# Half of a cosine FFN's first product by one level of Strassen's recursion, in pairs of token blocks

## The chip, the core and the metric

The kernel runs on one core of a Trainium2 chip. The time is the device time of one execution in microseconds (us). PE is TensorE's matrix multiplication (PEld its loading of weights), DVE is VectorE, ACT is ScalarE, POOL is GpSimd, and SP is SyncE, which issues most DMAs here. PSUM is the matmuls' output memory, of eight banks with 512 fp32 values for each of 128 partitions; SBUF is the working memory; DRAM here is the chip's own large memory. Matmul operands are fp32r, a shortened fp32 that TensorE multiplies in one pass.

## The reference

Sparse attention over 8 batches, 8 heads, 576 positions of 64 values, and a feed-forward part on its output of 4608 tokens by 512:

```python
scores = q @ k.T / sqrt(64)
mask_local   = (0 <= i - j) & (i - j < 32)        # heads 0 to 3
mask_strided = (0 <= i - j) & (i % 32 == j % 32)  # heads 4 to 7
attn = softmax(where(mask, scores, -1e9))
x = (attn @ v)           # heads side by side: 4608 x 512
h = x @ w_in             # 512 x 2048
g = h * cos(h)
out = g @ w_out          # 2048 x 512
```

## The kernel before

The feed-forward part works on blocks of 384 tokens, twelve in all (`j` from 0), and for each block on 16 chunks `f` of 128 hidden values. A step (`chunk(j, f)`) is one pair (block, chunk). Every fp32 operand is held as a high part, rounded to fp32r, and a low part, the rest; a product is high × high + low × high + high × low. `hidden` makes the first product: 4 slices of 128 inputs by 3 matmuls, twelve 384-wide matmuls into a bank `h` (L420). Then comes a chain that changes engines: ACT counts the turns of 2π (L426), DVE takes them off (L427), ACT makes the sine, with the quarter turn that makes a cosine of it (L430), DVE multiplies it by h (L433), ACT rounds the high part `g_hi` (L436), POOL takes the low part `g_lo` (L437). `outer` makes the second product: 3 tiles of 128 tokens by 3 matmuls, nine 512-wide matmuls into `acc0` to `acc2` (L444). It runs LAG = 3 steps behind `hidden`, so that the chain has three steps' time. After a block's last chunk ACT and DVE copy the three sums to `o` (L452, L454), and SP writes them out (L455).

All weights are converted at the start and in block 0 (L135 to L154) and stay in SBUF as `wi_h`, `wi_l`, `wo_h`, `wo_l`.

Attention is cut into units, seven a batch: three local ones (L277 scores, L286 a transpose on DVE, L298 products) and four strided ones (L328 scores, L344 transposes on PE, L358 products). The local products fill two banks, copied out by ACT (L306) and DVE (L310). Batches 0 and 1 come ahead of the feed-forward part and feed blocks 0 and 1 from SBUF. The 42 units of batches 2 to 7 are laid over the steps of blocks 2 to 11 by the table `KNOTS`; they write their result to `xT` in DRAM, from which `load_x` takes each later block (L399, split at L389 and L390). Two units' stretches make a `burst` ahead of a step's first product: the products of one unit and the scores of a later one, interleaved matmul by matmul where both use the same tile shape. Three banks (`acc0` to `acc2` of the pool `ps`) are attention's own, two are `h`'s, three are the sums'.

The matmuls of blocks 2 to 11 stand in the order in which they are written (`in_turn`); a scheduler sets the order of each other engine's queue at build time, and an engine takes its queue in that order. A DMA of SP waits in SP's queue until what it needs is there.

Of the kernel before, what the change touches and what calls it, by code (L numbers as in the profile page):

```python
# [74 lines left out]
def attention_cos_ffn(ctx, tc, qkl, vl, qkvs, w_in, w_out, eye, eye16, mask_l0, mask_l, mask_s, out):  # L75
# [40 lines left out]
    wi_h = const.tile([P, NFC, NKC, P], F32R, name="wi_h")  # L116
    wi_l = const.tile([P, NFC, NKC, P], F32R, name="wi_l")
    wo_h = const.tile([P, NFC, DM], F32R, name="wo_h")
    wo_l = const.tile([P, NFC, DM], F32R, name="wo_l")
# [59 lines left out]
    class Attention:  # L179
# [134 lines left out]
        def strided(self, b, p, u):  # L314
# [9 lines left out]
            mask = ms.unsqueeze(1).broadcast_to([P, SU, GB])  # L324
            s_ps = self.score_bank(mask)

            def score(t, i):
                self.scored = self.pe(nc.tensor.matmul(  # L328
                    s_ps[half(1 - i, GB), t * GB:(t + 1) * GB], q_t[half(i), t], k_t[half(i), t],
# [86 lines left out]
    def hidden(j, f, x_hi, x_lo):  # L416
        h = ps_h.tile([P, 512], F32, name="h")[:, :TB]
        ops = [(w, x, c) for c in range(NKC) for w, x in ((wi_h, x_hi), (wi_h, x_lo), (wi_l, x_hi))]
        for i, (w, x, c) in enumerate(ops):
            mm = nc.tensor.matmul(h, w[:, f, c], x[c], start=(i == 0), stop=(i == len(ops) - 1))  # L420
# [19 lines left out]
    def outer(j, f, g_hi, g_lo, acc):  # L440
        for t in range(NTT):
            ts = slice(t * P, (t + 1) * P)
            for i, (g, w) in enumerate(((g_hi, wo_h), (g_hi, wo_l), (g_lo, wo_h))):
                mm = nc.tensor.matmul(  # L444
                    acc[t], g[:, ts], w[:, f], start=(f == 0 and i == 0), stop=(f == NFC - 1 and i == 2)
# [228 lines left out]
```

## Time and profile before

| | |
|---|---|
| runs | 946.0, 948.48, 949.2 us; median 948.48 |
| profiled execution | span 945.8 us; the page gives its span only, and the fastest run, 946.0, is 0.2 us longer |
| PE | 928.2 us busy, 98% of the span, 8020 matmuls |
| PEld / ACT / DVE / POOL | 87% / 50% / 46% / 39% |
| DMA | 75.55 MB, 80 GB/s over the span |
| first products, L420 | 768 × 3 matmuls of 384 |
| second products, L444 | 576 × 3 matmuls of 512 |

A group's row reads: line, engine, operation, output<-inputs, shapes, xcount, then after the bar the busy time and the mean ns of one, then the idle time of that engine just ahead of them and what ended it. A row in order of time reads: start, duration, engine, line, operation, output<-inputs, and in brackets the idle time ahead of it and the instruction whose end released it. In a row by windows, the busy times of PE, PEld, DVE, ACT and POOL are followed by PEclk (the TensorE clock granted, 1 is full), the DMA engines' busy share, and GB/s. A DMA row ends with KB each and the median us from issue to landing.

### The profile page before, as it was taken

What the parts mean: (1) busy time and instruction counts of PE and PEld (TensorE: products, weight loads), DVE (VectorE), ACT (ScalarE), POOL (GpSimd) and SP (SyncE); (2) the same over time, 40 slices, a digit from 0 to 9 for tenths busy, and PEclk for the clock granted to TensorE, in tenths of its full rate; (3) what the DMA queues carried; (4) which work ended last, traced back from release to release, by engine and by line L of the source; (5) the groups of instructions that cost most, each with busy time, mean ns of one, the idle gap of its engine ahead of it and who ended that gap; (6) DMA issues with size and microseconds to landing.
All of it is one profiled execution on the core that took longest, in us unless ns stands there. A gap on an engine that the chain in (4) does not pass through costs nothing. (4 is left out here: it accounts for less than half of the span.)

```text
span 945.8 us, 19478 instructions
## 1 busy us (share of the span) xinstructions
PE 928.2 (98%) x8020; PEld 818.7 (87%) x8020; DVE 435.2 (46%) x885; ACT 468.8 (50%) x947; POOL 365.3 (39%) x382
## 2 busy tenths in 40 slices
PE   9899999999999999999999999999999999999998
PEld 5678899998888888888989888888998889999997
DVE  5657756446554444343344443534444444323222
ACT  3556777465555544545445543544445543433433
POOL 2636655535443353323343343423243334223221
PEclk9679999999999999999999999999999999999999
DMA  8634433123423222111213232112211311000000
GB/s 306 209 101 146 148 134 112 34 99 120 119 60 112 64 72 88 60 42 58 86 43 104 60 93 68 61 38 66 82 47 60 98 33 42 34 1 26 34 1 34
DMA packets 40265, 75.55 MB, mean 80 GB/s; under 512 B 4848, under 2 KB 22768, under 8 KB 40176
## 3 DMA queue, kind: packets, MB, share of 16 engines
q1 hardware_dynamic: 31680, 66.21, 22.2%
q10 hardware_dynamic: 8496, 8.09, 2.5%
q8 instruction: 63, 1.03, 0.5%
q14 instruction: 26, 0.21, 0.1%
HBM read 56.98 MB, written 17.30 MB: 79 GB/s over the span
## 5 line engine op out<-in xcount | busy, mean ns | idle before, releaser
L437 POOL TENSOR_TENSOR g_lo<-r,g_hi 128x384 fp32r<-128x384 f32 x192 | 198.9, 1036 | 439.0 <-issue 237.1
L420 PE MATMUL h<-x_hi,wi_h 128*128 128x384 f32 x768 | 264.2, 344 | 4.9 <-DVE r L433 4.8
L420 PE MATMUL h<-x_hi,wi_l 128*128 128x384 f32 x768 | 259.0, 337 | 0.0
L420 PE MATMUL h<-x_lo,wi_h 128*128 128x384 f32 x768 | 258.1, 336 | 0.0
L444 PE MATMUL acc<-wo_h,g_hi 128*128 128x512 f32 x576 | 228.1, 396 | 1.0 <-DVE o L452 1.0
L427 DVE SCALAR_TENSOR_TENSOR r<-r,h 128x384 f32<-128x384 int32 x192 | 105.7, 550 | 265.7 <-ACT r L426 265.5
L444 PE MATMUL acc<-wo_l,g_hi 128*128 128x512 f32 x576 | 226.7, 394 | 0.0
L444 PE MATMUL acc<-wo_h,g_lo 128*128 128x512 f32 x576 | 222.7, 389 | 0.0
L426 ACT ACTIVATE r<-h 128x384 int32<-128x384 f32 x192 | 93.4, 486 | 153.0 <-PE h L420 146.1
L430 ACT ACTIVATE r<-r,biases 128x384 f32<-128x384 f32 x192 | 118.3, 616 | 99.6 <-DVE r L427 97.9
L420 PEld LDWEIGHTS h<-x_hi,wi_h 128*128 128x128 f32 x768 | 144.4, 188 | 17.0 <-DVE r L433 7.8
L420 PEld LDWEIGHTS h<-x_lo,wi_h 128*128 128x128 f32 x768 | 144.5, 188 | 5.5
L436 ACT CAST g_hi<-r 128x384 fp32r<-128x384 f32 x192 | 98.4, 512 | 93.2 <-DVE r L433 91.9
L420 PEld LDWEIGHTS h<-x_hi,wi_l 128*128 128x128 f32 x768 | 144.2, 188 | 0.1
L433 DVE TENSOR_TENSOR r<-r,h 128x384 f32<-128x384 f32 x192 | 105.9, 552 | 81.9 <-ACT r L430 81.5
L444 PEld LDWEIGHTS acc<-wo_h,g_lo 128*128 128x128 f32 x576 | 108.1, 188 | 24.2
L444 PEld LDWEIGHTS acc<-wo_h,g_hi 128*128 128x128 f32 x576 | 108.0, 188 | 18.6 <-DVE o L452 1.8
L444 PEld LDWEIGHTS acc<-wo_l,g_hi 128*128 128x128 f32 x576 | 108.4, 188 | 14.7
L390 POOL TENSOR_TENSOR x_lo<-x_lo,x_hi 128x384 fp32r<-128x384 f32 x40 | 41.9, 1051 | 49.6 <-DVE x_hi L389 37.2
L242 ACT ACTIVATE e_sb<-t_sb,biases 128x324 f32<-128x324 f32 (+1 forms) x42 | 24.6, 586 | 57.7 <-POOL t_sb L233 42.7
L389 DVE CAST x_hi<-x_lo 128x384 fp32r<-128x384 f32 x40 | 22.7, 575 | 53.2 <-DMA x_lo<-xT 53.0
L233 POOL TENSOR_TENSOR t_sb<-t_sb,mx 128x324 f32<-128x324 f32 (+1 forms) x42 | 32.4, 771 | 18.3 <-DVE mx L232 18.3
(74 smaller groups left out, 737.6 us busy)
## 6 DMA issues: line engine op xcount, KB each, us to landing
qk<-in_qkvs SPq DMA_DIRECT2D x32, 324.0 KB, 3.7
qk<-in_qkl SPq DMA_DIRECT2D x24, 416.0 KB, 4.4
out<-o SPq DMA_DIRECT2D x36, 256.0 KB, 2.2
raw<-in_w_in SPq DMA_DIRECT2D x16, 512.0 KB, 4.3
raw<-in_w_out SPq DMA_DIRECT2D x16, 512.0 KB, 3.6
x_lo<-xT SPq DMA_DIRECT2D x40, 192.0 KB, 2.5
v<-in_vl SPq DMA_DIRECT2D x24, 224.0 KB, 3.1
xT<-x_l ACTq DMA_DIRECT2D x40, 96.0 KB, 3.0
```

Of the source, the lines that this page charges most:

```text
L233: nc.gpsimd.tensor_tensor(out=t, in0=t, in1=mx[:, :n].unsqueeze(2).broadcast_to([P, n, w]), op=ALU.subtract)
L242: nc.scalar.activation(out=e, in_=t, func=AF.Silu, bias=shift1, scale=0.0625)
L389: copy(out=hi, in_=x)
L390: nc.gpsimd.tensor_tensor(out=lo, in0=x, in1=hi.bitcast(F32), op=ALU.subtract)
L420: mm = nc.tensor.matmul(h, w[:, f, c], x[c], start=(i == 0), stop=(i == len(ops) - 1))
L426: nc.scalar.activation(out=k, in_=h, func=AF.Copy, scale=1.0 / (2.0 * math.pi), bias=0.25)
L427: red = nc.vector.scalar_tensor_tensor(out=r, in0=k, scalar=-2.0 * math.pi, in1=h, op0=ALU.mult, op1=ALU.add)
L430: sin = nc.scalar.activation(out=r, in_=r, func=AF.Sin, bias=quarter)
L433: nc.vector.tensor_tensor(out=r, in0=r, in1=h, op=ALU.mult)
L436: nc.scalar.copy(out=g_hi, in_=r)
L437: nc.gpsimd.tensor_tensor(out=g_lo, in0=r, in1=g_hi.bitcast(F32), op=ALU.subtract)
L444: mm = nc.tensor.matmul(acc[t], g[:, ts], w[:, f], start=(f == 0 and i == 0), stop=(f == NFC - 1 and i == 2))
```

## The change

Blocks 0 to 3 stay as they are (`PLAIN` = 4). Blocks 4 to 11 are worked off as four pairs. For a pair (2 × 384 tokens) and a "quad" q (chunks q and q + 8), the first product is a 2 × 2 product of blocks: hidden halves by input halves of 256, and input halves by token halves. One level of Strassen's recursion in Winograd's form makes it with 7 products in place of 8. Each is 2 slices by 3 matmuls, six 384-wide matmuls: 42 for a quad in place of 48.

- Seven combined weights are made for each of 8 quads, while blocks 2 and 3 run (`combine`): four are sums, made by POOL and DVE, split by ACT and POOL; three are plain ones. All, and `w_out`'s parts, are written to DRAM (`wis`, `wos`). In blocks 4 to 11 they are read back for each quad of each pair (`load_quad`, 2.88 MB), two quads ahead. The resident weights' memory is released at block 4.
- Seven combined token operands are made for each pair (`stage_x`) and split (`split_operand`: 14 casts on ACT, 7 subtractions each on DVE and POOL). For later pairs this lies in the last quad of the pair before.
- Six banks hold the pair's sums `acc0` to `acc5`, two (`a`, `b`) are left. The seven products accumulate in these; four results (c11, c22, c21, c12) leave them by an ACT copy or a DVE addition into SBUF and go through the same chain (`curved`).
- The second product's 12 outer tiles of the quad before (3 matmuls of 512 each) are put between the seven products, 2, 2, 2, 2, 2, 1 and 1 of them.
- Attention: batches 2 to 4 (21 units) and the two units in flight are laid over blocks 2 and 3 (16 burst slots in 16 steps, then 7 in 11). Batches 5 to 7 (21 units, 12 strided and 9 local) go one to a quad, in `a` and `b`: scores behind the third product, transposes ahead of the seventh, products at the end, each a stretch of its own.

```diff
-KNOTS = ((3, 0), (13, 9), (29, 15), (61, 23), (77, 29), (109, 37), (125, 43), (141, 44))
+KNOTS = ((3, 0), (19, 16), (30, 23))
+PLAIN = 4
+FILL = (2, 2, 2, 2, 2, 1, 1)
...
+    def combine(sp, q):
...
+        def formed(i, x, y, op):
+            t = sp.tile([P, 2 * P], F32, name="sf", bufs=3)
+            nc.vector.tensor_tensor(out=t, in0=x, in1=y, op=op)
+            part = sp.tile([P, 2, 2 * P], F32R, name="sr", bufs=2)
+            nc.scalar.copy(out=part[:, 0], in_=t)
+            nc.gpsimd.tensor_tensor(out=part[:, 1], in0=t, in1=part[:, 0].bitcast(F32), op=ALU.subtract)
+            nc.sync.dma_start(out=wis[q][i], in_=part.bitcast(F32))
...
+            if n >= LAG + 1 and (n - LAG - 1) % 3 == 0 and (n - LAG - 1) // 3 < NQ:
+                combine(sp, (n - LAG - 1) // 3)
         while pend:
             outer(*pend.pop(0))
+    plain.close()
...
+        def stage_x(c):
+            at = (PLAIN + 2 * c) * TB
+            held = {}
+            for name, k, n in (("b12", 0, 1), ("b11", 0, 0), ("b22", 1, 1), ("b21", 1, 0)):
+                held[name] = xr.tile([P, 2, TB], F32, name=name)
+                nc.sync.dma_start(out=held[name], in_=xT[:, 2 * k:2 * k + 2, at + n * TB:at + (n + 1) * TB])
+            b12, b11, b22, b21 = held.values()
+            t1, t2, t4 = (xr.tile([P, 2, TB], F32, name=name) for name in ("t1", "t2", "t4"))
+            nc.vector.tensor_tensor(out=t1, in0=b12, in1=b11, op=ALU.subtract)
+            nc.vector.tensor_tensor(out=t2, in0=b22, in1=t1, op=ALU.subtract)
+            nc.gpsimd.tensor_tensor(out=b12, in0=b22, in1=b12, op=ALU.subtract)
+            nc.gpsimd.tensor_tensor(out=t4, in0=b21, in1=t2, op=ALU.subtract)
+            return t2, b11, b21, b12, t1, t4, b22
+
+        def split_operand(i, raw):
+            hi, lo = (xo.tile([P, 2, TB], F32R, name=f"{name}{i}") for name in ("xo_hi", "xo_lo"))
+            for k in range(2):
+                nc.scalar.copy(out=hi[:, k], in_=raw[:, k])
+                engine = nc.vector if k else nc.gpsimd
+                engine.tensor_tensor(out=lo[:, k], in0=raw[:, k], in1=hi[:, k].bitcast(F32), op=ALU.subtract)
+            return hi, lo
+
+        def load_quad(q):
...
+                ws.append(wr.tile([P, 2, 2, P], F32R, name="wq", bufs=20))
...
+                wos_.append(wr.tile([P, 2, DM], F32R, name="wo", bufs=7))
...
+        def products(unit):
+            att.banks = [(ps, "a"), (ps, "b")]
...
+        raws = stage_x(0)
+        operands = [split_operand(i, raw) for i, raw in enumerate(raws)]
+        loaded = {n: load_quad(n % NQ) for n in range(2)}
+        for n in range(total):
...
+            last = q == NQ - 1 and c + 1 < NPAIR
+            if last:
+                raws = stage_x(c + 1)
+            def use(i, to, start, stop):
+                product(to, w[i], operands[i], start, stop)
+                if last:
+                    operands[i] = split_operand(i, raws[i])
+            b = bank("b")
+            use(0, b, True, False)
+            fill(FILL[0])
+            a = bank("a")
+            use(1, a, True, False)
+            nc.scalar.copy(out=p1, in_=a)
+            nc.vector.tensor_tensor(out=u2, in0=b, in1=p1, op=ALU.add)
+            fill(FILL[1])
+            use(2, a, False, True)
+            nc.scalar.copy(out=c11, in_=a)
+            made.append((q, 0, 0, curved(c11)))
+            fill(FILL[2])
+            if n < len(units):
+                scores(units[n])
+            use(3, b, False, False)
+            nc.vector.tensor_tensor(out=u3, in0=b, in1=p1, op=ALU.add)
+            fill(FILL[3])
+            a = bank("a")
+            use(4, a, True, False)
+            nc.vector.tensor_tensor(out=c22, in0=a, in1=u3, op=ALU.add)
+            made.append((q + NQ, 1, 1, curved(c22)))
+            fill(FILL[4])
+            use(5, b, False, True)
+            nc.vector.tensor_tensor(out=c21, in0=b, in1=p1, op=ALU.add)
+            made.append((q + NQ, 1, 0, curved(c21)))
+            fill(FILL[5])
+            if unit:
+                turned(unit)
+            use(6, a, False, True)
+            nc.vector.tensor_tensor(out=c12, in0=a, in1=u2, op=ALU.add)
+            made.append((q, 0, 1, curved(c12)))
+            fill(FILL[6])
+            if unit:
+                products(unit)
```

The order of the queues shows three places. In these rows a name's number tells buffers apart, and brackets give the semaphores waited for. First SP, at the step from one block to the next. Before, `out_0<-o` writes a block's sums and `x_lo<-xT` loads the operand of the block after next:

```order
L399 DMA x_lo_5019<-xT_96 128x384 [waits PE_49,Pool_49]
L399 DMA x_lo_5020<-xT_96 128x384 [waits DMAHW5_49,PE_49,Pool_49]
L268 DMA v_4344<-in_vl 128x448 [waits DMAHW6_49,PE_49]
L317 DMA qk_4735<-in_qkvs 128x648 [waits DMAHW3_49,DMAHW1_49,PE_49]
L399 DMA x_lo_5021<-xT_96 128x384 [waits DMAHW7_49,DMAHW2_49,Pool_49]
L399 DMA x_lo_5022<-xT_96 128x384 [waits DMAHW3_49,DMAHW0_49,Pool_49]
L455 DMA out_0<-o_4481 128x512 [waits DMAHW4_49,Activation_49]
L455 DMA out_0<-o_4487 128x512 [waits DMAHW5_49,DVE_49]
L455 DMA out_0<-o_4493 128x512 [waits DMAHW6_49,Activation_49]
```

In the changed kernel, at the step from block 3 to the first pair, `b12` to `b21` are the first pair's operands and `wq` its first weights:

```order
L282 DMA v_5687<-in_vl 128x448
L471 DMA out_0<-o_5108 128x512 [waits Activation_49]
L652 DMA b12_5167<-xT_159 128x2x384
L471 DMA out_0<-o_5114 128x512 [waits DVE_49]
L471 DMA out_0<-o_5120 128x512 [waits DMAHW2_49,Activation_49]
L652 DMA b11_5169<-xT_159 128x2x384 [waits DMAHW3_49]
L652 DMA b22_5171<-xT_159 128x2x384 [waits DMAHW4_49]
L652 DMA b21_5173<-xT_159 128x2x384 [waits DMAHW5_49]
L673 DMA wq_5224<-wis0_160 128x512 [waits DMAHW6_49]
```

Before, the loads of the next block's operand stand ahead of the writes of the sums; now three of the four stand behind them.

Second POOL, at a change of blocks. Before (`pn_s` and `t_sb` are a softmax's, L390 splits the next block's operand):

```order
L437 TENSOR_TENSOR g_lo_5962<-r_5956,g_hi_5961 128x384 [waits PE_49,Activation_49,Pool_49]
L437 TENSOR_TENSOR g_lo_5993<-r_5987,g_hi_5992 128x384 [waits PE_49,Activation_49,Pool_49]
L233 TENSOR_TENSOR t_sb_6033<-t_sb_6033,mx_6034 128x324 [waits DVE_49]
L437 TENSOR_TENSOR g_lo_6067<-r_6061,g_hi_6066 128x384 [waits PE_49,Activation_49,Pool_49]
L390 TENSOR_TENSOR x_lo_6692<-x_lo_6692,x_hi_6688 128x384 [waits DMAHW1_49,DVE_49]
L253 TENSOR_TENSOR pn_s1_89<-e_sb_6038,z_6043 128x6x54 [waits DVE_49]
L437 TENSOR_TENSOR g_lo_6107<-r_6101,g_hi_6106 128x384 [waits PE_49,Activation_49,Pool_49]
L437 TENSOR_TENSOR g_lo_6138<-r_6132,g_hi_6137 128x384 [waits PE_49,Activation_49,Pool_49]
```

After, at the step to the first pair (`xo_lo0` to `xo_lo6` are the low parts of the seven operands, `xo_lo0` that of the first product):

```order
L453 TENSOR_TENSOR g_lo_5044<-r_5038,g_hi_5043 128x384 [waits PE_49,Activation_49,Pool_49]
L453 TENSOR_TENSOR g_lo_5075<-r_5069,g_hi_5074 128x384 [waits PE_49,Activation_49,Pool_49]
L666 TENSOR_TENSOR xo_lo1_5189<-b11_5169,xo_hi1_5188 128x384 [waits DMAHW3_49,Activation_49]
L657 TENSOR_TENSOR b12_5167<-b22_5171,b12_5167 128x768 [waits DMAHW4_49,DMAHW0_49,DVE_49]
L666 TENSOR_TENSOR xo_lo4_5207<-t1_5175,xo_hi4_5206 128x384 [waits Activation_49]
L666 TENSOR_TENSOR xo_lo6_5219<-b22_5171,xo_hi6_5218 128x384 [waits Activation_49]
L658 TENSOR_TENSOR t4_5177<-b21_5173,t2_5176 128x768 [waits DMAHW5_49,DVE_49]
L666 TENSOR_TENSOR xo_lo2_5195<-b21_5173,xo_hi2_5194 128x384 [waits Activation_49]
L666 TENSOR_TENSOR xo_lo0_5183<-t2_5176,xo_hi0_5182 128x384 [waits Activation_49]
L666 TENSOR_TENSOR xo_lo3_5201<-b12_5167,xo_hi3_5200 128x384 [waits Activation_49]
L666 TENSOR_TENSOR xo_lo5_5213<-t4_5177,xo_hi5_5212 128x384 [waits Activation_49]
```

Before, one split of the next block's operand stands among the low parts `g_lo` of running steps; now nine operations stand in a row behind the last `g_lo`, and `xo_lo0` is the seventh of them.

Third DVE, where a local unit's products are copied out. Before (`x_l<-acc1` is the copy):

```order
L251 RECIPROCAL z_6043<-z_6043 128x6 [waits DVE_49]
L427 SCALAR_TENSOR_TENSOR r_6101<-r_6101,h_6088 128x384 [waits Activation_49,Pool_49]
L433 TENSOR_TENSOR r_6101<-r_6101,h_6088 128x384 [waits Activation_49]
L427 SCALAR_TENSOR_TENSOR r_6132<-r_6132,h_6119 128x384 [waits Activation_49]
L433 TENSOR_TENSOR r_6132<-r_6132,h_6119 128x384 [waits Activation_49]
L310 COPY x_l_6151<-acc1_6153 128x192 [waits DMAHW2_49,PE_49]
L231 TENSOR_TENSOR t_sb_6210<-acc0_2449,ml_75 128x384 [waits PE_49]
L232 TENSOR_REDUCE mx_6211<-t_sb_6210 128x6 [waits DVE_49]
```

After, in the last quad of a pair (L793 and L801 make c21 and c12, L693 and L695 are the chain's two DVE operations, `x_l<-b` is the copy):

```order
L793 TENSOR_TENSOR h_6619<-b_6476,p1_6496 128x384 [waits PE_49]
L695 TENSOR_TENSOR r_6598<-r_6598,h_6596 128x384 [waits Activation_49]
L264 TENSOR_SCALAR z_6569<-z_6569 128x6 [waits DVE_49]
L265 RECIPROCAL z_6569<-z_6569 128x6 [waits DVE_49]
L693 SCALAR_TENSOR_TENSOR r_6621<-r_6621,h_6619 128x384 [waits Activation_49,Pool_49]
L801 TENSOR_TENSOR h_6639<-a_6589,u2_6497 128x384 [waits PE_49]
L300 STREAM_TRANSPOSE pt_l_6574<-e_sb_6564 128x384 [waits Pool_49]
L695 TENSOR_TENSOR r_6621<-r_6621,h_6619 128x384 [waits Activation_49]
L693 SCALAR_TENSOR_TENSOR r_6641<-r_6641,h_6639 128x384 [waits Activation_49]
L695 TENSOR_TENSOR r_6641<-r_6641,h_6639 128x384 [waits Activation_49]
L324 COPY x_l_6654<-b_6656 128x192 [waits DMAHW6_49,PE_49]
```

In both the copy stands behind the multiply that follows a sine (L433, now L695 on c12's `r_6641`). Before, it empties a bank of attention's own; now it empties `b`, which the next quad's first product fills.

More of the change, by code (lines that the diff above doesn't have):

```diff
@@ L114, in order @@
         )
[L116 to L119, printed above, removed]
+    wp = plain.enter_context(tc.tile_pool(name="wp", bufs=1, reuse_waits="tile"))
+    wi_h, wi_l, wo_h, wo_l = [], [], [], []
+    for f in range(NFC):
+        for held, name, shape in (
+            (wi_h, "wi_h", [P, NKC, P]), (wi_l, "wi_l", [P, NKC, P]), (wo_h, "wo_h", [P, DM]), (wo_l, "wo_l", [P, DM]),
+        ):
+            held.append(wp.tile(shape, F32R, name=f"{name}{f}"))
+    xs = plain.enter_context(tc.tile_pool(name="xs", bufs=2 * NKC, reuse_waits="tile"))
     xT = dram.tile([P, NKC, NTOK], F32, name="xT")
+    wis = [dram.tile([7, P, 2, 2 * P], F32, name=f"wis{q}") for q in range(NQ)]
+    wos = [dram.tile([P, 2, DM], F32, name=f"wos{f}") for f in range(NFC)]
     def load_weight(cv, src, hi, lo, after, scalar):
@@ L162, in need_weights @@
             load_weight(
-                cv, w_in.bitcast(I32)[f], wi_h[:, f].rearrange("p c n -> p (c n)"),
-                wi_l[:, f].rearrange("p c n -> p (c n)"), after, False,
+                cv, w_in.bitcast(I32)[f], wi_h[f].rearrange("p c n -> p (c n)"),
+                wi_l[f].rearrange("p c n -> p (c n)"), after, False,
             )
-            load_weight(cv, w_out.bitcast(I32)[f], wo_h[:, f], wo_l[:, f], after, True)
+            load_weight(cv, w_out.bitcast(I32)[f], wo_h[f], wo_l[f], after, True)
             weights = f + 1
@@ L201, in bank @@
         def bank(self, kind):
-            pool, name = next(kind)
+            pool, name = self.banks.pop(0) if self.banks else next(kind)
             return pool.tile([P, 512], F32, name=name)
@@ L215, in score_bank @@
                 return bank
+            if self.banks:
+                return self.bank(None)
             n = next(self.turns)
@@ L324, in strided @@
             mask = ms.unsqueeze(1).broadcast_to([P, SU, GB])
+            rows = GP if self.banks else GB
             s_ps = self.score_bank(mask)
@@ L333, in strided @@
             yield [
-                partial(score, t, i) for t in range(SU) for i in range(2) if SU * u + t // 2 * 2 + i < NG
+                partial(score, t, i) for t in range(SU) for i in range(2)
+                if rows == GP or SU * u + t // 2 * 2 + i < NG
             ], "64x64"
@@ L419, in hidden @@
         for i, (w, x, c) in enumerate(ops):
-            mm = nc.tensor.matmul(h, w[:, f, c], x[c], start=(i == 0), stop=(i == len(ops) - 1))
+            mm = nc.tensor.matmul(h, w[f][:, c], x[c], start=(i == 0), stop=(i == len(ops) - 1))
             if j >= 2:
@@ L444, in outer @@
                 mm = nc.tensor.matmul(
-                    acc[t], g[:, ts], w[:, f], start=(f == 0 and i == 0), stop=(f == NFC - 1 and i == 2)
+                    acc[t], g[:, ts], w[f], start=(f == 0 and i == 0), stop=(f == NFC - 1 and i == 2)
                 )
@@ L563, in attention_cos_ffn @@
             )
[L564 removed]
+        for n in range(LAG, (PLAIN - 2) * NFC):
             j, f = 2 + n // NFC, n % NFC
```

143 lines of the change are left out of this document (129 added, 14 removed).

## The prediction

> **What bounds the kernel now.** I read the page first, then PE's waits, then the order in time of single steps, and last the PE stretches in which attention interrupts the products.
>
> ```profile
> span 945.8 us, 19478 instructions
> PE 928.2 (98%) x8020; PEld 818.7 (87%) x8020; DVE 435.2 (46%) x885; ACT 468.8 (50%) x947; POOL 365.3 (39%) x382
> ...
> PE h L420 <- DVE r L433: 4.8, 5, 1.6
> ```
>
> TensorE works in 98% of the span, and the largest of its waits (last row: total, times, longest) sum to under 5 us. So the time is the number of matmuls by their pace, and a change of the matmul count pays in full, unless it opens waits. The sum below is made against this execution of 945.8 us. The runs were 946.0, 948.48 and 949.2, so their median stands 2.7 us above it; I add the sum to the median.
>
> The pace and the chain behind one first product, in order of time (start, duration):
>
> ```profile
> 830.46 0.33 PE L420 MATMUL h<-x_hi,wi_h 128*128 128x384 f32 x1
> ...
> 832.39 0.34 PE L420 MATMUL h<-x_hi,wi_l 128*128 128x384 f32 x1
> 832.57 0.39 PE L444 MATMUL acc<-wo_h,g_hi 128*128 128x512 f32 x1
> 832.82 0.49 ACT L426 ACTIVATE r<-h 128x384 int32<-128x384 f32 x1 [1.30 <-PE h L420]
> 833.35 0.56 DVE L427 SCALAR_TENSOR_TENSOR r<-r,h 128x384 f32<-128x384 int32 x1 [2.37 <-ACT r L426]
> 833.94 0.62 ACT L430 ACTIVATE r<-r,biases 128x384 f32<-128x384 f32 x1 [0.62 <-DVE r L427]
> 834.59 0.55 DVE L433 TENSOR_TENSOR r<-r,h 128x384 f32<-128x384 f32 x1 [0.68 <-ACT r L430]
> 834.63 0.33 PE L420 MATMUL h<-x_hi,wi_h 128*128 128x384 f32 x1
> ```
>
> Twelve 384-wide matmuls take 832.57 − 830.46 = 2.11 us (0.1755 each); nine 512-wide ones take 834.63 − 832.57 = 2.06 (0.229 each). Starts count, since records overlap. A reader of a finished bank starts 832.82 − 832.57 = 0.25 us after PE's next slot. From the start of L426 to the end of L433 is 2.32 us.
>
> **The removed matmuls.** A pair of blocks had 2 × 16 × 12 = 384 matmuls in the first product; now 8 quads × 7 products × 6 = 336. The second product stays at 288. Four pairs save 192 × 0.1755 = 33.7 us, all on the path.
>
> **Attention alone in its stretches.** These rows price it:
>
> ```profile
> 204.00 0.34 PE L420 MATMUL h<-x_hi,wi_l 128*128 128x384 f32 x1
> 204.27 0.81 PE L328 MATMUL acc<-qk 64*54 64x54 f32 x24
> 205.00 0.44 PE L420 MATMUL h<-x_hi,wi_h 128*128 128x384 f32 x1
> ...
> 735.48 0.39 PE L444 MATMUL acc<-wo_h,g_lo 128*128 128x512 f32 x1
> 735.80 0.26 PE L358 MATMUL acc<-pt,v 54*64 54x54 f32 x1
> 735.80 0.25 PE L328 MATMUL acc<-qk 64*54 64x54 f32 x1
> ...
> 736.53 0.44 PE L420 MATMUL h<-x_hi,wi_h 128*128 128x384 f32 x1
> ...
> 787.43 0.39 PE L444 MATMUL acc<-wo_h,g_lo 128*128 128x512 f32 x1
> 787.74 1.02 PE L298 MATMUL acc<-pt_l,v 32*64 32x32 f32 x56
> 788.69 0.44 PE L420 MATMUL h<-x_hi,wi_h 128*128 128x384 f32 x1
> ```
>
> Strided scores alone cost 205.00 − 204.00 − 0.1755 = 0.82; strided scores and products interleaved cost 736.53 − 735.48 − 0.229 = 0.82 for both: the second rides free in the other part of the array. 17 of the 42 bursts from block 2 on are such pairs. Now each kind has its own stretch, so about 8.5 pairs, the half that lies in blocks 4 to 11, lose 0.9 each, 7.7; and about 12 more changes between kinds at 0.1 (the 0.1 by which a first matmul behind a stop runs longer, 0.44 for 0.33) give 1.2. **+8.9** (5 to 10).
>
> **Waits for the two banks.** 21 quads carry attention. c21's sum must leave bank b before transposes, and c12's must leave a before products; one outer tile (3 × 0.229 = 0.69) lies between. The reader needs 0.25 + 0.55 (DVE, L433's width) + 0.06 (DVE to PE, below) = 0.86, so 0.17 is bare: 12 strided units × 0.17 + 21 × 0.17 = 5.6, with 1.4 for a DVE found busy: **+7** (0 to 12).
>
> The nine local units are worse. Their products end the quad, and the next quad's first product goes to the same bank b. It is emptied by a DVE copy that stands in DVE's queue behind L695, the multiply after c12's sine (DVE is drawn in the order of the part on the change), and DVE takes its queue in order. Its row, and those that price the wait's two ends:
>
> ```profile
> L310 DVE COPY x_l<-acc 128x192 f32<-128x192 f32 x18 | 6.3, 352 | 8.0 <-PE acc L298 8.0
> ...
> 65.68 0.55 DVE L433 TENSOR_TENSOR r<-r,h 128x384 f32<-128x384 f32 x1 [0.40 <-ACT r L430]
> ...
> 66.29 0.44 PE L420 MATMUL h<-x_hi,wi_h 128*128 128x384 f32 x1 [1.58 <-DVE r L433]
> ```
>
> DVE to PE is 66.29 − (65.68 + 0.55) = 0.06. From the end of c12's product: 0.25 + 0.55 + 0.04 + 2.32 + 0.35 + 0.06 = 3.57. PE has 0.69 + 0.17 + 1.03 + 0.1 = 1.99 to do. 1.58 × 9 = **+14.2**. If the copy were free of the sine, the wait would be 0.25 + 0.35 + 0.06 ≈ 0.68, so 6.1; a late sine would make 20. The queue order is fixed, so I take 14.2.
>
> In the last quad of three pairs, ACT's split casts (14 × 0.5) stand ahead of the copies that empty bank a: two or three casts' delay, with one for c11, some 1.7 each: **+5** (0 to 10).
>
> **The join at block 4.** The seven operands of the first pair are built after the plain stage; nothing on PE covers them. Rows: tail of a block, loads, POOL, the clock.
>
> ```profile
> 941.72 0.39 PE L444 MATMUL acc<-wo_h,g_lo 128*128 128x512 f32 x1
> 942.14 0.58 ACT L454 COPY o<-acc 128x512 f32<-128x512 f32 x1 [0.79 <-PE acc L444]
> ...
> 0.74 0.39 SPq L317 DMA_DIRECT2D qk<-in_qkvs  x1
> 1.18 0.42 SPq L319 DMA_DIRECT2D v<-in_qkvs  x1
> ...
> qk<-in_qkl SPq DMA_DIRECT2D x24, 416.0 KB, 4.4
> ...
> L437 POOL TENSOR_TENSOR g_lo<-r,g_hi 128x384 fp32r<-128x384 f32 x192 | 198.9, 1036 | 439.0 <-issue 237.1 <-ACT g_hi L436 193.0 <-DMA out<-o 3.3
> L154 POOL TENSOR_TENSOR wo_l<-bits,wo_h 128x512 fp32r<-128x512 f32 x16 | 20.9, 1305 | 1.3 <-ACT wo_h L153 1.3
> ...
> 47.00:48.00 1.00, 0.45 (x2) 0.45 (x3) 0.49 (x1) 0.47 (x2) 1.00 (x2) 0.50 0.43 153
> 59.00:60.00 1.00, 1.00 (x4) 0.67 (x3) 0.57 (x1) 0.00 (x0) 0.00 (x0) 0.50 0.33 105
> 60.00:61.00 1.00, 1.00 (x57) 0.90 (x56) 0.00 (x0) 0.00 (x0) 0.00 (x0) 0.82 0.33 105
> 65.00:66.00 1.00, 0.00 (x0) 0.00 (x0) 0.60 (x2) 0.99 (x3) 0.00 (x0) 1.00 0.00 0
> ```
>
> From the last plain matmul's start T0, the output copy ends at T0 + 1.0. On SP the loads of b11, b22, b21 stand behind the output copies, 0.45 apart (rows of SP); b22 is out at about T0 + 1.7 and lands 4.4 later (416 KB row; it has 384), T0 + 6.1 with the queue's reaction. POOL then works off six or seven operations in order, low parts at 1.05 and 768-wide sums at 1.85 (1.036 at 384 and 1.305 at 512 wide extrapolated), and the one that the first product needs is the seventh: lo1 1.05 (until T0 + 7.4), b12 1.85, lo4 1.05, lo6 1.05, t4 1.85, lo2 1.05, lo0 1.05: T0 + 15. PE stands for some 15 us. Then the clock: in the windows rows (PEclk is the third number from the end), it fell to 0.50 around an idle stretch and came back some 2.3 us into the dense work (0.82 in 60:61), so half of 2.3, with a little more for the first quad's thin start, is 1.4. That quad has no tiles to fill between products; its copies of p1 and c11 lie bare, 1.9. **+18.3** (8, if the loads run ahead and POOL alone is left, to 24).
>
> **The rest.** Blocks 2 and 3 take 23 bursts where 16 stood, plus 8 combines. Per combine POOL gets 2 × 1.3 + 4 × 0.65, DVE and ACT four short ones each; all three were about half busy, so I cost them at **+3** (0 to 8): what would go late first is g_lo on POOL, and behind it the outer product. Plain weights' copies to DRAM are added to SP's queue in the start and blocks 0 and 1, between loads: **+1.5** (−1 to 4). The streamed weights are 2.88 MB per quad (7 × 256 KB and 2 × 512 KB). A quad lasts 42 × 0.1755 + 36 × 0.229 = 15.6 us and some 3 of attention and waits, so they need 155 GB/s, issued two quads ahead; cost nothing, covered by these capacities:
>
> ```profile
> 4.00:8.00 4.00, 4.00 (x36) 1.75 (x34) 0.99 (x2) 1.56 (x2) 0.00 (x0) 1.00 1.00 334
> 60.00:120.00 60.00, 56.80 (x336) 50.86 (x336) 43.63 (x66) 43.37 (x82) 33.46 (x27) 1.00 0.45 149
> ```
>
> 334 GB/s at full share, and 149 at 0.45. The output's last copies are as before.
>
> Sum: −33.7 + 8.9 + 7 + 14.2 + 5 + 18.3 + 3 + 1.5 = +24.2; 948.48 + 24.2 = 973. With the ends above taken as independent, the likeliest case lies in 955 to 990.
>
> **The rivals.**
> - The waits for banks are covered, and it gets faster. ACT and DVE are half busy; if the casts, copies and sums always come first, 7, 14.2, 5 and the first quad's 1.9 fall away: −3.9, so 944.6. It decides when all bank waits together come to less than 1 us (under −0.3%). Covered by part they give 946 to 954. For it: the 46% and 50%. Against: the order of the queues is fixed, and 1.58 us is worked out from durations. Chance 0.20 (faster 0.12, within 0.3% 0.08).
> - The clock. 21 quads with several short stops could drop the clock each time: 2.3 us at half speed is 1.15 lost, × 21 = 24, so 997. Against it: a stop of 1.58 us ended at 66.29 with the clock at 1.00 (row 65:66). Chance 0.06. The Trainium skill, "TensorE: Matmul & The Clock Gate", section "A second HAM failure mode: psum-queue depth-cycling", speaks for this rival: cycling through PSUM banks makes TensorE idle briefly so often that the clock swings between half and full. By it the time would be about 997; the one comparable stop in this trace does not show it, so my sum goes by the trace.
> - The weights come late. If one landing of 4.4 us lay bare in each of 31 quads, +136, so some 1100. For it: nine transfers a quad wait for free buffers; against: share 0.45 at that rate. Chance 0.04.
> - The forecast, slower by waits and join: 0.70.
>
> **The numbers.** About 0.3% (2.8 us) is what a measurement here tells from no change: 945.6 to 951.3. Faster 0.12 and within 0.08 come from the first rival; slower 0.80 is 0.70 + 0.06 + 0.04. The range 948 to 995 leaves out nearly all of the faster cases and the late stream with half of the clock's, near 0.2.
>
> **What would show it.** After: matmuls of the first product at 0.1755 and 33.7 us fewer of them; a PE idle stretch near 15 us where the stages join, released by POOL; waits near 1.6 us of first products on DVE's copy in nine quads; PEclk at 9 or more elsewhere. A join under 8 us, or waits under 0.3 us at the local quads, would make me wrong on the high side; PEclk below 9 in the later slices, or PE waiting for DMA, on the low side.

## The result, and the profile after

The changed kernel takes 1028.61 us (median of 4 runs, 1028.17 to 1029.69), the kernel before on the same chip 947.38: ratio 1.085, 95% interval 1.083 to 1.087. Slower was forecast, by 24 us; it is 81, outside the range.

From the page of the changed kernel:

```profile
span 1026.6 us, 20627 instructions
...
PE 933.2 (91%) x7852; PEld 806.1 (79%) x7852; DVE 584.6 (57%) x1085; ACT 533.2 (52%) x1095; POOL 438.9 (43%) x434
...
PEclk9899999999899996899989899999999989999999
```

TensorE is busy for about the same time (933.2 us for 928.2) with fewer matmuls (7852 for 8020), and it stands still for 9% of the span; its clock is no longer full throughout. Its largest waits (total, times, longest):

```profile
PE b L684 <- DVE x_l L324: 23.5, 9, 3.6
PE b L684 <- ACT xo_hi L664: 12.3, 1, 12.3
PE acc L360 <- DVE x_l L324: 12.0, 3, 6.6
PE a L684 <- DVE t_sb L245: 7.0, 3, 3.2
```

In order of time, a quad with a strided unit's scores, transposes and products in stretches of their own, and two late quads without attention:

```profile
420.78 0.33 PE L684 MATMUL b<-xo_hi,wq 128*128 128x384 f32 x1
...
428.16 0.91 PE L343 MATMUL a<-qk 64*64 64x54 f32 x24
...
435.83 0.55 PE L360 MATMUL b<-ident,pn_s 128*128 128x128 f32 x3
...
438.17 0.91 PE L374 MATMUL a<-pt,v 54*64 54x54 f32 x24
439.00 0.44 PE L684 MATMUL b<-xo_hi,wq 128*128 128x384 f32 x1
...
903.89 0.34 PE L684 MATMUL b<-xo_hi,wq 128*128 128x384 f32 x1
...
919.56 0.33 PE L684 MATMUL b<-xo_hi,wq 128*128 128x384 f32 x1
```

A quad alone takes 15.67 us, where four steps before took 4 × 4.17 = 16.68. Over 32 quads that is 32 us, so the 33.7 us forecast for the matmuls are nearly all there. A unit of attention adds 18.22 − 15.67 = 2.55; before, the time of blocks 2 to 10 beyond 16 steps each came to 74.9 us for 42 units, 1.78 each. By stretches, from the starts of first products (blocks 2 and 3 of before with the three second products that are still to come at block 4's start, 6.2 us):

| stretch | before | after | difference |
|---|---|---|---|
| until the feed-forward part starts | 58.2 | 54.0 | −4.2 |
| blocks 0 and 1 | 135.5 | 137.2 | +1.7 |
| blocks 2 and 3, to their last second product | 164.1 | 196.6 | +32.5 (12 of it the 7 units moved ahead, at 1.78) |
| join and quads (before: blocks 4 to 11) | 584.1 | 634.1 | +50.0 |
| tail | 3.9 | 4.7 | +0.8 |

The quads lose at the nine local units. This is one of them (PE, ACT, POOL and DVE):

```profile
475.16 0.22 PE L312 MATMUL b<-pt_l,v 32*64 32x32 f32 x2
...
475.75 0.61 ACT L694 ACTIVATE r<-r,biases 128x384 f32<-128x384 f32 x1
...
475.93 0.99 POOL L699 TENSOR_TENSOR g_lo<-r,g_hi 128x384 fp32r<-128x384 f32 x1 [1.09 <-ACT g_hi L698]
...
476.40 0.94 DVE L695 TENSOR_TENSOR r<-r,h 128x384 f32<-128x384 f32 x1 [0.68 <-ACT r L694]
477.26 0.34 DVE L324 COPY x_l<-b 128x192 f32<-128x192 f32 x1
...
477.66 0.44 PE L684 MATMUL b<-xo_hi,wq 128*128 128x384 f32 x1 [2.27 <-DVE x_l L324]
```

The copy waits for the multiply behind c12's sine, as forecast, and the multiply takes 0.94 us, not 0.55. It began while POOL was at L699 and ended 0.42 us after it (477.34 and 476.92). That is the rule in this trace. L695 reads two inputs from SBUF; L801, the sum c12, reads one of its two from PSUM (durations in ns, least, median and longest):

```profile
L695 DVE TENSOR_TENSOR r<-r,h x128: 509/558/1432, 416.2 to 1015.7; 128x384 f32<-128x384 f32 x128
...
L801 DVE TENSOR_TENSOR h<-a,u x32: 544/558/559, 421.0 to 1013.2; 128x384 f32<-128x384 f32 x32
```

Of the 128 L695, 58 began while POOL had more than 0.15 us of an operation left. All of them ended 0.41 to 0.42 us after that operation, after 0.59 to 1.43 us; the other 70 took 0.51 to 0.56. L801 began beside POOL's work in the same way 26 times and never took more than 0.56. The clock after this wait and after one of 3.01 us (at 541.20), by windows:

```profile
478.00:481.00 3.00, 3.00 (x17) 2.75 (x16) 0.00 (x0) 0.00 (x0) 1.01 (x1) 1.00 0.48 134
542.00:545.00 3.00, 3.00 (x11) 2.67 (x11) 0.52 (x1) 0.92 (x2) 1.45 (x2) 0.61 0.20 62
```

11 matmuls in 3 us at a clock of 0.61, for 17 at 1.00. From quad 1 on there are nine such drops, 3.4 us at half clock each or twice that; weighted by PE's busy share they cost some 19 us.

At the change to the second pair DVE stands at the next pair's first sum, and the scores' reader queues behind it:

```profile
523.88 0.96 DVE L655 TENSOR_TENSOR t<-b,b 128x768 f32<-128x768 f32 x1 [4.84 <-DMA wq<-wis]
...
527.83 0.55 DVE L245 TENSOR_TENSOR t_sb<-a,ml 128x384 f32<-128x384 f32 x1
...
528.43 0.69 PE L684 MATMUL a<-xo_hi,wq 128*128 128x384 f32 x1 [3.23 <-DVE t_sb L245]
```

The first row names a load of weights as what ended the wait, but what the sum needs is the load of `b` that SP issued at 520.30; it landed at 523.86.

The join (SP, DVE, POOL, PE):

```profile
389.12 1.99 SPq L652 DMA_DIRECT2D b<-xT  x3
...
394.91 0.96 DVE L655 TENSOR_TENSOR t<-b,b 128x768 f32<-128x768 f32 x1 [6.92 <-DMA b<-xT]
...
396.69 2.12 POOL L657 TENSOR_TENSOR b<-b,b 128x768 f32<-128x768 f32 x1
...
397.06 2.56 DVE L656 TENSOR_TENSOR t<-b,t 128x768 f32<-128x768 f32 x1
...
400.22 0.69 PE L684 MATMUL b<-xo_hi,wq 128*128 128x384 f32 x1 [12.27 <-ACT xo_hi L664]
...
406.42 0.69 PE L684 MATMUL b<-xo_lo,wq 128*128 128x384 f32 x1 [5.51 <-POOL xo_lo L666]
```

And block 2, where DVE stands at a split of the next block's operand and the copy of attention's bank queues behind:

```profile
266.71 0.36 DVE L405 CAST x_hi<-x_lo 128x384 fp32r<-128x384 f32 x1 [3.63 <-DMA x_lo<-xT]
...
271.53 0.33 DVE L324 COPY x_l<-acc 128x192 f32<-128x192 f32 x1
...
272.00 0.45 PE L360 MATMUL acc<-ident,pn_s 128*128 128x128 f32 x1 [6.57 <-DVE x_l L324]
```

### The profile page after: what moved, and what is told of

It is laid out like the page before. It is cut to its first block, busy times and chain, and to the rows that moved or that the text cites. A ratio compares the mean times of both kernels' runs of the same rounds, so it can differ in the third digit from the quotient of the medians.

```text
span 1026.6 us, 20627 instructions
## 1 busy us (share of the span) xinstructions
PE 933.2 (91%) x7852; PEld 806.1 (79%) x7852; DVE 584.6 (57%) x1085; ACT 533.2 (52%) x1095; POOL 438.9 (43%) x434
## 5 line engine op out<-in xcount | busy, mean ns | idle before, releaser
L712 PE MATMUL acc<-wo,g_hi 128*128 128x512 f32 x768 | 246.8, 404 | 0.0
L699 POOL TENSOR_TENSOR g_lo<-r,g_hi 128x384 fp32r<-128x384 f32 x128 | 133.4, 1043 | 232.6 <-ACT g_hi L698 120.8
L684 PE MATMUL a<-xo_hi,wq 128*128 128x384 f32 x512 | 158.3, 350 | 8.4 <-DVE t_sb L245 7.0
L712 PEld LDWEIGHTS acc<-wo,g_hi 128*128 128x128 f32 x768 | 146.5, 194 | 15.1
L684 PE MATMUL b<-xo_hi,wq 128*128 128x384 f32 x384 | 124.0, 364 | 35.8 <-DVE x_l L324 23.5
L712 PE MATMUL acc<-wo,g_lo 128*128 128x512 f32 x384 | 153.2, 399 | 0.0
L693 DVE SCALAR_TENSOR_TENSOR r<-r,h 128x384 f32<-128x384 int32 x128 | 81.2, 634 | 76.2 <-ACT r L692 75.1
L695 DVE TENSOR_TENSOR r<-r,h 128x384 f32<-128x384 f32 x128 | 85.7, 670 | 29.0 <-ACT r L694 27.5
L436 PE MATMUL h<-x_hi,wi_h 128*128 128x384 f32 x256 | 89.1, 348 | 3.2 <-DVE r L449 3.1
L436 PE MATMUL h<-x_hi,wi_l 128*128 128x384 f32 x256 | 86.3, 337 | 0.0
L436 PE MATMUL h<-x_lo,wi_h 128*128 128x384 f32 x256 | 85.9, 336 | 0.0
L460 PE MATMUL acc<-wo_h,g_hi 128*128 128x512 f32 x192 | 77.7, 405 | 0.0
L460 PE MATMUL acc<-wo_l,g_hi 128*128 128x512 f32 x192 | 77.0, 401 | 0.0
L460 PE MATMUL acc<-wo_h,g_lo 128*128 128x512 f32 x192 | 74.6, 396 | 0.0
```

The lines of the kernel that those rows point to most:

```text
L436: mm = nc.tensor.matmul(h, w[f][:, c], x[c], start=(i == 0), stop=(i == len(ops) - 1))
L460: mm = nc.tensor.matmul(acc[t], g[:, ts], w[f], start=(f == 0 and i == 0), stop=(f == NFC - 1 and i == 2))
L684: in_turn(nc.tensor.matmul(bank, w[:, n, c], part[:, c], start=start and i == 0, stop=stop and i == len(ops) - 1, skip_group_check=True,))
L693: nc.vector.scalar_tensor_tensor(out=r, in0=k, scalar=-2.0 * math.pi, in1=h, op0=ALU.mult, op1=ALU.add)
L695: nc.vector.tensor_tensor(out=r, in0=r, in1=h, op=ALU.mult)
L699: nc.gpsimd.tensor_tensor(out=g_lo, in0=r, in1=g_hi.bitcast(F32), op=ALU.subtract)
```

## The experiments

Each stands beside a run of the kernel before on the same chip: 949.5 us for e1 to e4, 947.9 for e5 to e8, 950.3 for e9 to e12. Each is one run, compared with the changed kernel's 1028.6, so a difference of 1 or 2 us between them says nothing.

**e1, the copy ahead of c12's chain.**

```diff
-            made.append((q, 0, 1, curved(c12)))
             fill(FILL[6])
             fill(len(fillers))
             if unit:
                 products(unit)
+            made.append((q, 0, 1, curved(c12, att.copied)))
```

(`curved` orders its first DVE step behind the copy that it is given.)

> Edit: in the quads, c12's chain is written behind attention's products, and its first DVE step is put behind the copy of bank b, so that the copy no longer stands behind c12's sine. Theory (a queue's head holds up the bank): the nine waits of the next quad's first product, 2.2 to 3.6 us each and 23.5 in all, fall below 0.9 each, and the drops of the clock that follow them (seven of the nine in the quads, 1.7 to 3.4 us each) go too: 1028.6 - 16 - 12, about 1000 us. Rival (the clock falls through the many short stops as such, whatever their length): the waits shrink but the clock still falls: about 1013. Second rival (the products themselves are late, DVE is too full): the wait stays over 1.5 us, 1022 or more.

1010.2 us, −18.5. The waits and the end of the same local unit:

```profile
PE b L684 <- DVE x_l L324: 9.8, 9, 2.3
...
477.07 0.36 DVE L324 COPY x_l<-b 128x192 f32<-128x192 f32 x1 [0.23 <-PE b L312]
...
477.48 0.45 PE L684 MATMUL b<-xo_hi,wq 128*128 128x384 f32 x1 [0.50 <-DVE x_l L324]
```

The wait of 2.27 is 0.50, the nine together 9.8 for 23.5, and the clock lost in the quads (half of the time at half clock) fell from 20.5 to 8.5 us. Quads 1 to 21 take 410.4 for 433.1. The time lies nearer to the first rival's 1013 than to the theory's 1000, but the drops decide: none is left behind the seven waits that fell to 1.6 us or less, and the four that stayed stand at waits of 1.8 to 4.6 us at the pair changes. So the theory holds in kind, with a smaller gain.

**e2, the next pair's sums held until the last quad.**

```diff
+            order(first_sum, after, "in the last quad")   # t1, after the c12 sum of the quad before
```

> Edit: the next pair's first DVE sum (L655) is held behind the c12 sum of the quad before the pair's last, so that it does not stand in DVE's queue while its load is under way. Theory: in quads 6, 13 and 20 DVE no longer stands 3 to 5 us at that sum; the three waits for scores (7.0 us) and two drops of the clock (3.4 and 1.7) go: 1028.6 - 10, about 1018 us, with the transposes' and products' waits near them a little shorter. Rival (the sums' own length, and DVE and POOL working at once, make the wait): the waits move to the last quad of the pair and the time stays within 4 us of 1028.6.

1028.1 us: no gain, so the rival holds. The wait for scores is gone from the list, and others grew:

```profile
PE b L686 <- DVE x_l L324: 27.9, 9, 5.5
...
PE a L686 <- ACT p L774: 4.8, 3, 3.5
```

The sums now stand in the quad that also has the 14 splits.

**e3, the four sums left out.** Plain weights are written in their place.

```diff
-        s1 = formed(4, a21, a22, ALU.add)
-        s2 = formed(0, s1, a11, ALU.subtract)
-        formed(3, a11, a21, ALU.subtract)
-        formed(6, a12, s2, ALU.subtract)
-        for i, f, k in ((1, q, 0), (2, q, 1), (5, q + NQ, 1)):
+        for i, f, k in ((4, q, 0), (0, q, 1), (3, q + NQ, 0), (6, q + NQ, 1), (1, q, 0), (2, q, 1), (5, q + NQ, 1)):
```

> Edit: in blocks 2 and 3 the four summed weights of each quad are left out; plain weights are copied in their place, so the DMA traffic stays and the output is not the reference's. Theory (writes of sums wait at the head of SP's queue, loads of x stand behind them, DVE waits for those): most of the 17 us of stops in blocks 2 and 3 go, and their drops of the clock (6.8): 1028.6 - 18, about 1010 us. Rival (21 units in two blocks are too dense by themselves): the stops stay, at most 5 us are won: 1024 or more.

1015.0 us, −13.6. Block 2 takes 96.0 us for 108.4, block 3 stays (89.3 for 88.2), and the wait of the transposes halves:

```profile
PE acc L360 <- DVE x_l L324: 5.6, 3, 3.0
```

Together the two blocks win 11 us. So of the 20 us that they lose beyond the moved units, some 11 go with the sums. The other 9 are left for the denser attention and the rest; no run took these apart.

**e4, the first pair's operands made in block 3.**

```diff
+        wp = plain.enter_context(tc.tile_pool(name=f"wp{f}", bufs=1, reuse_waits="tile"))   # one for each f
...
+        with tc.high_priority(offset=600):
+            raws = stage_x(0)
+            operands = [split_operand(i, raw) for i, raw in enumerate(raws)]
```

> Edit: the resident weights lie in one pool for each chunk, and the first pair's loads, sums and splits are written with a higher priority, so that they stand in block 3 ahead of the last outputs. Theory: TensorE's stop of 18 us at the join falls below 2, and the half clock behind it goes; 1028.6 - 18 - 5, about 1005 us, if block 3 takes the 24 split operations without a stop. Rival (the work only moves; DVE and POOL hold up block 3's own chain): half is given back, 1015 to 1020.

1024.1 us, −4.5, less than either expected. The join and the first quad fell from 33.0 to 21.2 us, but block 3 grew by 5.8 and the weights became late:

```profile
PE h L436 <- DVE r L449: 6.0, 3, 2.6
...
397.67 0.41 PE L684 MATMUL b<-xo_hi,wq 128*128 128x384 f32 x1 [2.95 <-DMA wq<-wis]
...
401.41 0.66 PE L684 MATMUL a<-xo_hi,wq 128*128 128x384 f32 x1 [2.20 <-DMA wq<-wis]
```

The splits came in one row in DVE's and POOL's queues and held up block 3's chains; the weights, which had been there before the operands, are now what ends the wait.

**e5, no attention in the quads.**

```diff
-        units = [unit for b in range(PB, B) for unit in att.units(b)]
+        units = []
...
-            at = (PLAIN + 2 * c) * TB
+            at = PLAIN * TB     # in stage_x
```

> Edit: the 21 units of attention are left out of the quads, and every pair works on the first pair's tokens (so that nothing unwritten is read); the output is not the reference's. Theory (attention in the two banks makes the loss of the quads): quads 1 to 21 go from 433 us to 21 x 15.7 = 330, so about 922 us with the join as it is; the clock stays full in the quads. Rival (the seven products in two banks, the streamed weights or the pair changes stop TensorE by themselves): quads over 16.5 us, 940 us or more.

936.1 us, −92.6. Of this, 37 us (21 × 1.78) is what these units cost in the kernel before; the other 55 came on top of it here. Quads inside a pair take 15.7 us. Quads 1 to 21 sum to 340.5, 11 over 21 × 15.67, most of it at the pair changes, where ACT's casts stand ahead of the copy p1:

```profile
PE a L684 <- ACT p L772: 7.8, 8, 2.1
```

Without attention, the seven products in two banks and the streamed weights cost nothing inside a pair. The theory holds, with 11 us of the rival's pair changes. The run takes out attention whole, so it does not tell its waits for the two banks from its own work on the engines.

**e6, twelve plain blocks**, with the `KNOTS` of the kernel before.

```diff
-PLAIN = 4
+PLAIN = NTB
```

> Edit: PLAIN = 12, all attention as in the kernel before and no combined weights: what is left of the change are weights in one tile per chunk and pools that wait tile by tile. Theory: the feed-forward part starts some 4 us earlier, as the changed kernel's did (54.0 for 58.2), and the rest is as before: 948.5 - 4, about 944 us. Rival: the earlier start comes from other luck in the order and is given back in block 0: 947 to 949.

948.1 us beside 947.9: the rival holds. The feed-forward part starts at 54.4 us for 58.2, block 0 takes 70.6 for 68.9 and block 2 85.8 for 83.2. The new pools neither cost nor win.

**e7, the sums written by POOL.**

```diff
-            nc.sync.dma_start(out=wis[q][i], in_=part.bitcast(F32))
+            nc.gpsimd.dma_start(out=wis[q][i], in_=part.bitcast(F32))
```

> Edit: POOL in place of SP issues the writes of the summed weights to DRAM, so no load of x stands behind them on SP. Theory: the stops of blocks 2 and 3 (17 us) halve, since leaving the sums out altogether won 13.6 us; 1028.6 - 8, about 1020 us. Rival (the sums' own work on DVE and POOL is what costs): within 3 us of 1028.6, or slower by POOL's issuing.

1037.5 us, 9 slower. Block 2 gained 7 us and block 3 lost 12. The same eight sums on DVE, first in the changed kernel, then here:

```profile
L531 DVE TENSOR_TENSOR sf<-wf,sf 128x256 f32<-128x256 f32 x8 | 5.7, 710 | 1.1 <-POOL sr L534 1.0
```

```profile
L531 DVE TENSOR_TENSOR sf<-wf,sf 128x256 f32<-128x256 f32 x8 | 8.9, 1107 | 0.0
```

They grew by half, but the other 24 of the 32 sums kept their length (724 ns and 726, 775 and 793), so this is 3 us. What in it made block 3 12 us longer is open.

**e8, e10, e11: the repairs together.** e1's copy; the next pair's sums behind c21 in the quad before the last; 4 of 7 second halves of the splits on DVE; e4's pools, with the first pair's casts ordered behind the sines of block 3's last seven steps, and its weights loaded early; and one tile put behind attention's products. e8 also has e7's writes; e10 writes by SP; e11 writes by SP two steps later. Of the edits not shown yet:

```diff
-                engine = nc.vector if k else nc.gpsimd
+                engine = nc.vector if k and i % 2 == 0 else nc.gpsimd
...
-FILL = (2, 2, 2, 2, 2, 1, 1)
+FILL = (1, 2, 2, 2, 2, 1, 1)
...
-            fill(len(fillers))
             if unit:
                 products(unit)
+            fill(len(fillers))
```

> Edit: the copy of bank b ahead of c12's chain (as before in e1), the next pair's sums behind c21 in the quad before the last, fewer of the splits on DVE (4 of 7 second halves), resident weights in a pool for each chunk with the first pair's operands spread over block 3's last steps and its weights loaded early, writes of the sums issued by POOL, and one outer tile put behind attention's products. Theory (each loss is a queue's head): 1028.6 - 18 (quads) - 18 (join) - 8 (blocks 2 and 3) - 8 (tile behind products, sums), about 977 us; still over the kernel before, as attention stands unpaired. Rival (DVE and POOL are too full, stops only move): 995 or more.

> Edit: as e8, but SP issues the sums' writes as the changed kernel does (POOL's issuing made e7 9 us slower). Theory: blocks 2 and 3 take 197 us again where e8 took 209.5: 992.4 - 12, about 980 us. Rival (the spread splits of the first pair, not POOL's issuing, made block 3 longer): 988 or more.

> Edit: as e10, and each quad's four sums are written to DRAM two steps after they are made (four buffers for them in place of two), so that the writes do not wait at the head of SP's queue. Theory: most of what leaving out the sums won in block 2 (12 us) comes: about 970 us. Rival (the sums' 14 operations per quad on DVE, ACT and POOL are what costs): within 4 us of e10.

992.4, 979.0 and 981.2 us. e8 came nearer to its rival. It differs from e10 in the issuing engine alone; e10's blocks 2 and 3 take 197.3, e8's 209.4, so POOL's issuing was the 12. e11 won nothing, but it does not settle what holds block 2, because the writes stayed at SP's head for most of their wait (SP's waits for the sums, e10 and then e11):

```profile
SPq L537 <- POOL sr L536: 54.2, 29, 4.6
```

```profile
SPq L526 <- POOL sr L543: 42.5, 28, 4.0
```

In e7, where SP waited for no sum, block 2 was 7 us shorter. So how the sums' 11 us divide between their work and their writes is open. e10's join and first quad take 13.3 us for 33.0 and its quads 1 to 21 397.4 for 433.1. The largest of PE's waits that is left:

```profile
PE acc L360 <- DVE x_l L324: 12.3, 3, 7.2
```

Against the kernel before, e10's span of 977.2 is 31.4 longer: 33.2 in blocks 2 and 3 (12 of it moved work), −0.9 in all that follows up to the last matmul, −0.9 in the rest.

**e9, stops made on purpose in the kernel before.**

```diff
+        if j >= 6 and f % 4 == 2:
+            touch(ident16)                       # a small matmul into the bank's unused part
+            nc.vector.tensor_copy(out=x[:64, :P], in_=bank[:64, TB:])
+            for n, wide in enumerate(STOPS[(4 * j + f // 4) % len(STOPS)]):
...
+            touch(x.bitcast(BF16)[:, :P])        # a small matmul that waits for the chain
```

> Edit: the kernel before, with 24 stops of TensorE made on purpose in blocks 6 to 11: at the start of every fourth step a small matmul, a DVE chain of 0 to 4 operations on its result, and a second small matmul that waits for it; seven lengths, about 0.6 to 3 us. Theory (the length of a single stop decides): stops under 1.8 us leave the granted clock at 1, those over 2.5 us are followed by some 3.4 us at half clock, between them some are. Rival (the clock falls by the number of stops close to each other, as cycling of banks would have it): drops do not sort by length. In time about 948 + 24 x 1.7 + 7 x 1.7, 1000 us.

1047.1 us. A short and a long stop, and the three us near behind each:

```profile
654.05 0.22 PE L422 MATMUL h<-idle,warm 128*64 128x128 bf16 x1 [1.30 <-DVE idle L431]
...
901.86 0.27 PE L422 MATMUL h<-idle,warm 128*64 128x128 bf16 x1 [3.48 <-DVE idle L431]
```

```profile
654.00:657.00 3.00, 2.95 (x16) 2.72 (x16) 1.40 (x3) 0.46 (x2) 1.75 (x2) 1.00 0.00 0
903.00:906.00 3.00, 3.00 (x11) 3.00 (x10) 0.00 (x0) 0.00 (x0) 0.00 (x0) 0.50 0.00 0
```

| length of the stop, us | stops | followed by half clock |
|---|---|---|
| up to 1.4 | 7 | 0 |
| 1.98 to 2.90 | 8 | 5 |
| 2.91 to 6.4 | 9 | 9 |

So the drops sort by length at both ends of the table, but not between: a stop of 1.98 us dropped the clock, and stops of 2.71 and 2.90 did not. The traces show what decides there. In both kernels' traces and in e9's, every change of the clock stands on a grid of 3.41 us. In the changed kernel, from 60 us on, each of the 14 grid windows at full clock in which PE was busy for 0.47 or less was followed by half clock, and none of the 244 in which it was busy for 0.52 or more. In e9 the two sides are 0.46 or less (15 windows) and 0.55 or more (254). Over all fourteen traces the line lies between 0.44 and 0.57. Two local units with waits of 2.27 us each show it, the one at 477.66 and one at 769.24 (changed kernel; the row 478:481 above has the full clock behind the first):

```profile
476.11:479.52 3.41, 1.86 (x10) 1.74 (x11) 1.21 (x2) 0.97 (x3) 1.82 (x2) 1.00 0.63 216
766.24:769.65 3.41, 1.14 (x50) 1.03 (x47) 2.26 (x4) 2.20 (x5) 1.23 (x3) 1.00 0.85 312
769.65:773.06 3.41, 3.41 (x11) 3.02 (x10) 0.00 (x0) 0.00 (x0) 0.94 (x1) 0.50 0.35 88
```

The first stop was split between two windows and left 1.86 of 3.41 us busy, the second left 1.14. So length sorts only where a stop is too short to leave a window half idle, or too long to be split so evenly. And the rival is right where short stops share a window, as in e8, where stops of 1.61 and 1.73 us lie in one with 1.31 and 1.21 us:

```profile
335.24:338.65 3.41, 0.89 (x40) 0.77 (x40) 1.11 (x3) 2.45 (x6) 2.72 (x4) 1.00 0.06 14
338.65:342.06 3.41, 2.89 (x9) 2.89 (x10) 2.07 (x6) 1.37 (x4) 2.36 (x3) 0.50 0.97 295
```

**e12, six plain blocks and three pairs**, with e10's repairs.

```diff
-PLAIN = 4
+PLAIN = 6
-KNOTS = ((3, 0), (19, 16), (30, 23))
+KNOTS = ((3, 0), (13, 9), (29, 15), (62, 31))
```

> Edit: as e10, with six plain blocks and three pairs (PLAIN = 6), the sums at every sixth step, and 29 units of attention laid over blocks 2 to 5 at about the pace of the kernel before, 13 in the quads. Theory (density in blocks 2 and 3 costs more than a fourth pair saves, which is 8.4 us): blocks 2 to 5 near 330 us, quads 15.7 us and 2.6 more with a unit, so about 955 us, near the kernel before. Rival (pairs are worth having wherever they stand): 975 or more, since one pair fewer saves less.

972.6 us, 6 less than e10, and between the theory's 955 and the rival's 975, nearer to the rival's. That the density costs more than the fourth pair saves fits this, but is not shown: the run also spreads the sums over twice as many steps and has eight units fewer in the quads. Blocks 2 to 5 take 339 us for the 330 expected, and quads 1 to 21, of which 13 carry a unit, 376.6 where 21 × 15.67 + 13 × 2.55 = 362 was. No version tried that has pairs and does all the work is faster than the kernel before.

## Why the prediction was wrong

The direction stood, and so did most mechanisms. Two steps failed outright: the clock in the quads was put at nothing and cost 19 us, and blocks 2 and 3 were put at 3 us, because their engines were half busy, and cost 20. Four more terms were too small: attention alone, the copy at the local units, the pair changes and the join. By its steps, in us:

| term | forecast | measured | from |
|---|---|---|---|
| matmuls | −33.7 | −32 | 32 × (16.68 − 15.67) |
| attention alone | +8.9 | +16 | 21 × (2.55 − 1.78) |
| c21's and c12's sums | +7 | +4 | PE's waits for L793 and L801 |
| the copy at local units | +14.2 | +23.5 | 9 waits |
| pair changes | +5 | +9 | waits for scores 7.0, for p1 and casts 2 |
| join | +18.3 | +25 | stop 12.4; first quad 20.6 where 8.2 is work |
| blocks 2 and 3 | +3 | +20 | 32.5 less 12 moved |
| start, blocks 0 and 1 | +1.5 | −2.5 | |
| clock in the quads | 0 (a rival, chance 0.06) | +19 | nine drops |

These sum to 82, with the tail's 0.8 to 83, for 80.8 measured; stops and half clock overlap a little.

- **The clock.** The rival was turned down because a stop of 1.58 us had left the clock at 1.00. It had: the row 65:66 ends before that stop does, but the clock of that trace stays at 1.00 from 60.4 to 944 us. Yet the stop left its window of 3.41 us only 54% busy, close to the line that e9 and the changed kernel show. The waits forecast at 1.58 became 2.2 to 3.6, and seven of the nine crossed that line. That the rival's 24 us come near the measured 19 is luck: it reckoned with 21 drops of 1.15 us, and nine of about 2 came. The Trainium skill, "TensorE: Matmul & The Clock Gate", section "A second HAM failure mode: psum-queue depth-cycling", blames frequent short idles at bank changes; the drops here follow the idle share of a window, which mostly one stop filled, and the page's effect, the clock swinging, came about.
- **The copy.** The order of the queue was read rightly; the durations were taken from a chain whose `h` lies in PSUM. Here `h` is an SBUF tile, so L695 reads two SBUF inputs, and when it begins beside an operation of POOL it ends only 0.41 to 0.42 us behind that (58 of 58). The Trainium skill, "GPSIMD Engine Reference", section "1. Specifications", says that POOL shares its SBUF interfaces with VectorE and that DVE instructions with two SBUF inputs contend for them; the traces agree. The waiting goes by who begins first: at the join POOL's L657 began first, and DVE's 768-wide L656 took 2.56 us; at the three pair changes L656 took 0.96 although POOL worked beside it, and POOL's L657, which began 0.04 us after it, took 2.57 to 2.62 for 2.12.
- **The join.** Same order, same waits; the first sum starts only at T0 + 7.3 (394.91 − 387.56), when its operands land, and POOL's first seven operations take 11.2 us for the 8.95 reckoned: 18 us of stop for 15. The first quad, with no tiles between its products, then ran nearly whole at half clock.
- **Blocks 2 and 3.** "All three were about half busy" was the failing step: a share does not say what stands at the head of a queue. DVE's stood 3.63 us at a split whose load was late, and TensorE 6.57 us (rows at 266.71 and 272.00). e3 gives the sums some 11 us; how the other 9 divide is open.
- **Pair changes.** The casts ahead of the copies that empty bank a were seen, and cost 2 of the 9 us here (without attention, in e5, the pair changes cost most of 11). The other 7 come from what was not seen: the scheduler puts the next pair's first sum into DVE's queue where its load has not landed (row at 523.88).
- **Attention alone.** The loss by unpairing was counted (17 pairs of 42 bursts), at 0.4 a unit; it came to 0.8. That each of three stretches pays its entry and exit would explain the rest, but no run shows it by itself.
- The streamed weights cost nothing, as forecast (e5), and the rival of late weights fell: no wait of TensorE for them stands among those of the changed kernel.

## What to carry to other kernels

When a change puts more users on a shared buffer, price each wait from the queue that frees it: what stands at that queue's head, and whether its input is there in time. Take the durations from operations with the same kinds of operands. Then ask how much of a clock window the wait leaves idle: where that is about half, it costs more than its own time. An engine half busy on average is no cover.
